# Three score tiles per burst beside denominators and values in a fused attention and FFN kernel

## The chip, the cores and the metric

The kernel runs on one core of one Trainium2 chip. The metric is the device time of one execution in microseconds (us), the median over several runs. The core has five engines with instruction queues of their own: TensorE (PE: matmuls, and PEld: its weight loads), VectorE (DVE), ScalarE (ACT), GpSimd (POOL) and SyncE (SP, which issues transfers). Each works through its own queue in order and waits on semaphores for the others.

## The reference

Attention with normalised queries and keys, and then a two-layer network with a leaky unit:

```python
q_n, k_n = rmsnorm(q, g_q), rmsnorm(k, g_k)          # x / sqrt(mean(x*x) + 1e-6) * g
scores = q_n @ k_n.T / sqrt(64)                      # per batch and head
attn   = softmax(scores)                             # over keys
x      = attn @ v            # -> (8*448, 12*64) tokens x model
h      = x @ w_in                                    # 768 -> 2048
g      = maximum(h, 0) + alpha * minimum(h, 0)
out    = g @ w_out                                   # 2048 -> 768
```

Sizes: 8 batches, 12 heads, 448 positions, 64 values per head; 3584 tokens, model width 768, inner width 2048. Inputs and output are float32 in memory; the matmuls run on float16.

## The kernel before

**Groups and tiles.** Four heads make a group `y`, so a batch has 3 groups (`G`) and the kernel 24 (`NG`). The 448 keys of a group are cut into 7 tiles of 64 (`J`). `score(y, j)` (L184) computes one score tile: four 64x64 matmuls that run side by side on quarters of the array, into a PSUM tile `sc` of which there are two. `soft(y, j)` (L198) is its exponential on ACT, from PSUM to `expT`.

**Around a group.** `load_qk` fetches queries and keys. `square` (L120; POOL, for the first two groups ACT), `reduce` (L130; DVE), `root` (L138; two small ACT instructions) and `scale` (L147; POOL, three of them on DVE) normalise them. `turn` (L157) transposes them on PE into the PSUM tile `acc`, and two DVE copies take them to `qT` and `kT`. When all seven tiles of a group are exponentiated, `den` (L221) sums them over keys by 28 matmuls with ones, into `acc`; `log` and `invert` (L225, L230) on ACT make the reciprocal. `attv` (L234) multiplies by the values, 28 matmuls into `acc` again, and a DVE multiply (L240) writes `xT`. There is a single `acc` buffer for turns, denominators and values.

**The network.** For every batch there are 16 `up` units (L245: six matmuls into a PSUM tile `hT`, then `ah` on ACT at L257 and `gT` on DVE at L258) and, per two batches, 14 `down` units (L262: sixteen matmuls into `op`, a DVE copy to `osb`, every second one with two output transfers on SP). `hT` and `op` share two PSUM buffers. A `down` can carry `jobs`, which it issues between its matmuls and its copy.

**The order.** Everything is issued in an order written out by hand (`tc.manual_schedule()`), so the loop at L413 decides each engine's queue. The loop runs over bursts `n`. A burst scores two tiles; in the burst after a group's last tile it also does that group's denominators, in the next one its values:

```python
dens = {last(y) + 1: y for y in range(NG)}
avs = {last(y) + 2: y for y in range(NG)}
```

Behind the matmuls of a burst stand its exponentials, the logarithm, roots and scales that are due (`roots`), a turn (`turns`), and then `gaps[n]`: the ups and downs that a small planner (L343 to L377) puts there. It goes by fixed costs per unit (`UP`, `DOWN`) and per burst (`cost(n)`). `invert` is issued behind the burst's second up. `prep` and `post` hold loads, squares and reduces by burst. Before the first batch's values are complete there are no ups; there `spin` (L284) issues idle matmuls in place of them, four in a plain burst and one in others. What is left after the last burst is in `rest`.

Of the kernel before, what the change touches and what calls it, by code (L numbers as in the profile page):

```python
# [21 lines left out]
def kernel(  # L22
# [14 lines left out]
    B, H, S, D = q.shape  # L37
    DM = H * D
    DF = moe_w_in.shape[1]
    J = S // 64  # L40
    HH = H // 2
    G = HH // 2
# [4 lines left out]
    NG = B * G  # L47
# [59 lines left out]
    def load_w_in(c):  # L107
        nc.gpsimd.dma_start(
            out=w_in_sb[:, :, ts(c, FB)],
            in_=moe_w_in[:, ts(c, FB)].rearrange("(k p) f -> p k f", p=128),  # L110
        )
# [45 lines left out]
    def turn(y):  # L157

        ps = psa.tile([128, 2, 512], FP32, name="tps", tag="acc")
        tps = [  # L160
            ps[:, n, : S].bitcast(FP16).rearrange("p (j c) -> p j c", j=J)
            for n in range(2)
        ]
        for tp, nm in zip(tps, "qk"):
            for j in range(J):
                nc.tensor.transpose(  # L166
                    tp[:, j, :], qs[y, nm][:, j].rearrange("p h d -> p (h d)"), ident
                )
        for tp, nm in zip(tps, "qk"):
            t = att.tile([128, 2, J, 64], FP16, name=f"{nm}T", tag=f"{nm}T", bufs=3)  # L170
            o = t.rearrange("p g j c -> p j g c")
            i4 = tp.rearrange("p j (g c) -> p j g c", g=2)
            if nm == "q":
                nc.vector.tensor_copy(out=o, in_=i4)
            else:
                nc.vector.tensor_scalar(  # L176
                    out=o, in0=i4, scalar1=gain[:, 0:1], scalar2=None, op0=ALU.mult
                )
            qkT[y, nm] = t
# [4 lines left out]
    def score(y, j):  # L184
        qT, kT = qkT[y, "q"], qkT[y, "k"]
        sc = pss.tile([128, 2, 512], FP32, name="sc", tag="sc")
        for par in range(2):
            for g in range(2):
                nc.tensor.matmul(  # L189
                    out=sc[ds(64 * g, 64), par, :S],  # L190
                    lhsT=kT[ds(64 * par, 64), g, j, :],
                    rhs=qT[ds(64 * par, 64), g].rearrange("p j c -> p (j c)"),
                    start=True,
                    stop=True,
                )
        scs[y, j] = sc

    def soft(y, j):  # L198
        if j == 0:
            expT[y] = att.tile([128, J, 2, S], FP16, name="expT", tag="expT")  # L200
        nc.scalar.activation(  # L201
            out=expT[y][:, j], in_=scs[y, j][:, :, :S], func=AF.Exp,
            scale=QK_SCALE, bias=expb[:, 0:1],
        )
# [16 lines left out]
    def den(y):  # L221
        dn = over_keys("dn", y, lambda g, par, j: ones[ds(64 * g, 64), :])
        rden[y] = dn

    def log(y):  # L225
        r = att.tile([128, 2, S], FP32, name="rden", tag="rden")
        nc.scalar.activation(out=r, in_=rden[y][:, :, :S], func=AF.Ln)  # L227
        rden[y] = r
# [5 lines left out]
    def attv(y):  # L234
        b, i = divmod(y, G)
        vv = vt[b]
        av = over_keys("av", y, lambda g, par, j: vv[ds(64 * g, 64), 2 * i + par, j, :])
        if i == 0:
            xT[b] = att.tile([128, 2, G, S], FP16, name="xT", tag="xT")
        nc.vector.tensor_mul(  # L240
            out=xT[b][:, :, i, :], in0=av[:, :, :S], in1=rden[y]
        )
# [41 lines left out]
    def spin(count):  # L284

        if count:
            ps = psf.tile([128, 512], FP32, name="spin", tag="mm")
            for _ in range(count):
                nc.tensor.matmul(  # L289
                    out=ps[:, :S], lhsT=ident, rhs=idle, start=True, stop=True  # L290
                )
# [1 line left out]

    NB = (NG * J + 1) // 2

    def last(y):
        return (J * y + J - 1) // 2

    dens = {last(y) + 1: y for y in range(NG)}
    avs = {last(y) + 2: y for y in range(NG)}
    prep, post, roots = {}, {}, {}

    def at(n, f, *a):
        prep.setdefault(max(int(n), 0), []).append((f, a))

    def after(n, f, *a):
        post.setdefault(max(int(n), 0), []).append((f, a))

    turn_at = [J * y // 2 - 1 for y in range(NG)]
    turns = {n: y for y, n in enumerate(turn_at) if y}
    jobs = {}
    for y in range(G, NG):

        n = turn_at[y - 1] if y < G + 2 else last(y - G) + 2
        at(n - 8, load_qk, y)
        for nm in "qk":
            at(n - 2, square, y, nm)
            if y < G + 2:  # L320
                after(n, reduce, y, nm)
            else:
                jobs.setdefault(n, []).append((reduce, (y, nm)))
        roots[n + 1] = y
    for b in range(1, B):
        at(J * G * b / 2 - 4, load_v, b)


    UP, DOWN = 1.13, 2.6
# [2 lines left out]
    for b in range(B):  # L332
        ups = [(UP, up, (b, ft)) for ft in range(NF)]
        odd = b % 2
        new = [
            (DOWN, down, (b - odd, t, oh))
            for t in (range(3, J) if odd else range(3)) for oh in range(2)
        ]
        tail = len(new) if b == B - 1 else 2 + odd
        periods.append((ups, carry, new[:tail]))  # L340
        carry = new[tail:]

    def cost(n):  # L343
        return 0.75 + (1.35 if n in dens or n in avs else 0.0) + (0.9 if n in turns else 0.0)

    first = last(G - 1) + 2
    gaps = [[] for _ in range(NB + 2)]
    for b in range(B - 1):
        lo = last(G * b + G - 1) + 2
        hi = last(G * b + 2 * G - 1) + 2  # L350
        ups, old, new = (list(u) for u in periods[b])
        mlp = sum(u[0] for u in ups + old + new)
        per = (mlp + sum(cost(n) for n in range(lo, hi))) / (hi - lo)
        clock = 0.0
        for n in range(lo, hi):
            clock += cost(n)
            free = n in avs or n in turns
            while ups or old or new:
                if old and (free or not ups):
                    u = old.pop(0)  # L360
                elif ups:
                    u = ups.pop(0)
                else:
                    u = new.pop(0)
                gaps[n].append(u[1:])
                clock += u[0]
                free = False
                ahead = 0.5 * (UP if ups else DOWN)
                if n < hi - 1 and clock + ahead > per * (n - lo + 1):
                    break  # L370
    ups, old, new = periods[B - 1]
    rest = []
# [30 lines left out]
                reduce(y, nm)  # L403
    for c in range(4):
        load_w_in(c)
        at(8 + 2 * c, load_w_out, c)
    after(0, root, 1)
    for nm in "qk":
        after(0, scale, 1, nm)
        after(2, reduce, 2, nm)  # L410
    roots[3] = 2

    for n in range(NB + 2):  # L413
        for f, a in prep.get(n, ()):
            f(*a)
        tiles = [divmod(m, J) for m in (2 * n, 2 * n + 1) if m < NG * J]
        for t in tiles:
            score(*t)
        if n in dens:
            den(dens[n])  # L420
        if n in avs:
            attv(avs[n])

        plain = n not in dens and n not in avs and n not in turns
        wait = plain and gaps[n] and gaps[n][0][0] is up
        late = []
        for t in tiles[:1] if wait else tiles:
            soft(*t)
        if wait:
            late = [(1, soft, t) for t in tiles[1:]]  # L430
        if n in dens:
            log(dens[n])
            late = [(2, invert, (dens[n],))]
        if n in roots:
            y = roots[n]
            root(y)
            for nm in "qk":
                scale(y, nm)
        if n in turns:
            turn(turns[n])  # L440
        done = 0
        for f, a in gaps[n]:
            if f is down:
                down(*a, jobs.pop(n, ()))
            else:
                f(*a)
                done += 1
                if late and done == late[0][0]:
                    for _, g, c in late:
                        g(*c)  # L450
                    late = []
        for _, g, c in late:
            g(*c)
        if n < first:
            spin(4 if plain else 1)
        for f, a in jobs.pop(n, []) + post.get(n, []):
            f(*a)
    for f, a in rest:
# [31 lines left out]
```

## Time and profile before

| | |
|---|---|
| median of 6 runs | 483.55 us (482.03 to 484.67) |
| the profiled execution's own time | 484.84 us |
| its span, first to last instruction | 483.1 us |
| PE matmul busy | 452.7 us, 4074 matmuls |
| ACT busy | 289.2 us; exponentials 160.3 us (168 of 1003 ns) |
| DVE busy | 217.2 us |
| POOL busy | 167.0 us |
| mean granted TensorE clock | 0.985 |
| first `up` starts | 51.86 us |

Durations that the profile gives for matmuls overlap, as they are pipelined: the distance from one start to the next is what one of them costs. "Idle before, releaser" names what ended an engine's wait.

### The profile page before, as it was taken

The page shows a single profiled execution, that of the slowest core. Times are in us where ns is not written, and L with a number is a line of the kernel's source. Part 1 is how long each engine was busy: PE and PEld are TensorE (multiplying, and loading weights), DVE is VectorE, ACT ScalarE, POOL GpSimd, SP SyncE. Part 2 cuts the span into 40 slices and gives each one's busy share as a digit, 9 for nine tenths or more (in the row PEclk, how much of TensorE's full clock was granted, in tenths as well). Part 3 has the DMA queues.
Part 4 walks back from the last instruction along what each step waited for, and adds up shares of the span by engine and source line. Part 5 has one row for each costly group of instructions (what it writes and reads, how often), then busy time and mean ns, then how long its engine had stood idle before and what let it go on. Part 6 is the DMA issues. An engine that isn't in the chain of part 4 may idle for free.

```text
span 483.1 us, 9494 instructions
## 1 busy us (share of the span) xinstructions
PE 452.7 (94%) x4074; PEld 235.4 (49%) x4074; DVE 217.2 (45%) x312; ACT 289.2 (60%) x399; POOL 167.0 (35%) x123
## 2 busy tenths in 40 slices
PE   6778899999999999999999999999999999999995
PEld 3243444555445454555545554554545554555463
DVE  2843554455354455355363353554462443334421
ACT  3788788757755756656764757558675558423300
POOL 3677636552352260541532442522613200000000
PEclk9797999999999999999999999999999999999999
DMA  7999997250705344423704425414501110111122
GB/s 191 197 256 228 239 215 135 62 142 18 168 0 122 99 110 58 110 66 79 156 11 110 110 74 95 106 43 103 92 1 34 35 34 1 34 34 33 34 65 66
DMA packets 32187, 45.46 MB, mean 94 GB/s; under 512 B 5008, under 2 KB 28560, under 8 KB 32144
## 3 DMA queue, kind: packets, MB, share of 16 engines
q1 hardware_dynamic: 19792, 32.13, 25.5%
q0 software_dynamic: 11776, 11.80, 15.6%
q10 hardware_dynamic: 576, 0.92, 0.6%
q8 instruction: 32, 0.52, 0.5%
q14 instruction: 11, 0.09, 0.1%
HBM read 45.62 MB, written 11.01 MB: 117 GB/s over the span
## 4 chain that ended last, share of the span: by engine, by line
PE 70%; ACT 12%; DVE 8%; issue 4%; POOL 3%; DMA 2%; SPq 0%; POOLq 0%; DVEq 0%; ACTq 0%
PE op L266 30%; PE hT L249 19%; PE sc L189 6%; ACT ah L257 6%; PE av L212 6%; PE dn L212 5%; DVE gT L258 4%; ACT expT L201 3%; DVE ss L133 3%; PE tps L166 3%; DMA nat<-in_k_dram 2%; POOL sq L127 1%; POOL qs L150 1%; PE spin L289 1%; ACT rden L227 1%
## 5 line engine op out<-in xcount | busy, mean ns | idle before, releaser
L201 ACT ACTIVATE expT<-sc,expb 128x896 f16<-128x896 f32 x168 | 160.3, 1003 | 51.2 <-PE sc L189 51.1
L249 PE MATMUL hT<-xT,w_in_sb 128*128 128x448 f16 x768 | 159.9, 353 | 8.0 <-DVE gT L258 6.5
L266 PE MATMUL op<-w_out_sb,gT 128*128 128x384 f16 x896 | 153.4, 327 | 1.7 <-DVE gT L258 1.7
L257 ACT ACTIVATE ah<-hT,alpha_sb 128x448 f16<-128x448 f32 x128 | 80.6, 634 | 97.3 <-PE hT L249 96.4
L258 DVE TENSOR_TENSOR gT<-hT,ah 128x448 f16<-128x448 f32 x128 | 79.5, 624 | 123.5 <-ACT ah L257 123.2
L150 POOL TENSOR_TENSOR qs<-nat,rr 128x896 f16<-128x896 f32 x45 | 75.0, 1687 | 128.9 <-ACT rr L145 105.1
L266 PEld LDWEIGHTS <-gT 128*128 128x128 f16 x896 | 85.1, 98 | 64.4 <-issue 11.2
L249 PEld LDWEIGHTS <-w_in_sb 128*128 128x128 f16 x768 | 72.4, 97 | 86.0 <-issue 26.2
L127 POOL TENSOR_TENSOR sq<-nat 128x896 f32<-128x896 f32 x44 | 72.9, 1677 | 86.8 <-DVE ss L133 86.8
L278 DVE COPY osb<-op 128x384 f32<-128x384 f32 x56 | 31.1, 555 | 86.6 <-PE op L266 86.6
L189 PE MATMUL sc<-qT,kT 64*64 64x448 f16 x672 | 52.2, 375 | 9.0 <-DVE kT L176 4.1
L133 DVE TENSOR_REDUCE ss<-sq 128x14 f32<-128x896 f32 x48 | 49.7, 1076 | 8.1 <-ACT sq L125 8.1
L240 DVE TENSOR_TENSOR xT<-av,rden 128x896 f16<-128x896 f32 x24 | 26.2, 1091 | 31.0 <-PE av L212 31.0
L212 PE MATMUL av<-expT,vt 64*64 64x448 f16 x672 | 36.0, 350 | 1.1 <-ACT rden L227 1.1
L212 PE MATMUL dn<-expT,ones 64*64 64x448 f16 x672 | 36.9, 356 | 0.0
L189 PEld LDWEIGHTS <-kT 64*64 64x64 f16 x672 | 13.8, 106 | 42.1 <-issue 31.8
L166 PE MATMUL tps<-ident,qs 128*128 128x128 f16 x336 | 23.7, 222 | 4.0 <-POOL qs L150 3.6
L212 PEld LDWEIGHTS <-vt 64*64 64x64 f16 x672 | 20.0, 107 | 13.4 <-issue 2.2
L212 PEld LDWEIGHTS <-ones 64*64 64x64 f16 x672 | 20.2, 110 | 12.9 <-issue 1.7
L166 PEld LDWEIGHTS <-qs 128*128 128x128 f16 x336 | 19.1, 99 | 12.9 <-issue 5.6
L227 ACT ACTIVATE rden<-dn 128x896 f32<-128x896 f32 x24 | 22.1, 920 | 4.2 <-PE dn L212 4.2
L232 ACT ACTIVATE rden<-rden 128x896 f32<-128x896 f32 x24 | 22.6, 943 | 0.3
(25 smaller groups left out, 98.9 us busy)
## 6 DMA issues: line engine op xcount, KB each, us to landing
out_dram<-osb SPq DMA_DIRECT2D x56, 192.0 KB, 2.7
nat<-in_q_dram SPq DMA_DIRECT2D x46, 224.0 KB, 3.9
nat<-in_k_dram SPq DMA_DIRECT2D x46, 224.0 KB, 5.0
vt<-in_v_dram POOLq DMA_DIRECT2D x16, 336.0 KB, 5.5
w_in_sb<-in_moe_w_in_dram POOLq DMA_DIRECT2D x4, 768.0 KB, 18.7
w_out_sb<-in_moe_w_out_dram POOLq DMA_DIRECT2D x4, 768.0 KB, 14.2
nat<-in_q_dram ACTq DMA_DIRECT2D x2, 224.0 KB, 6.4
nat<-in_k_dram ACTq DMA_DIRECT2D x2, 224.0 KB, 8.0
```

Source lines behind the costliest of these rows:

```text
L127: nc.gpsimd.tensor_mul(out=sqf, in0=src, in1=src)
L133: nc.vector.tensor_reduce(out=ss_t[y][:, "qk".index(nm)].rearrange("p h j -> p (h j)").unsqueeze(2), in_=sqs[y, nm], axis=AXIS_X, op=ALU.add,)
L150: eng.tensor_mul(out=t.rearrange("p j h d -> p h j d"), in0=nat[y, nm], in1=rr_t[y][:, "qk".index(nm)].unsqueeze(3).broadcast_to((128, 2, ...
L166: nc.tensor.transpose(tp[:, j, :], qs[y, nm][:, j].rearrange("p h d -> p (h d)"), ident)
L189: nc.tensor.matmul(out=sc[ds(64 * g, 64), par, :S], lhsT=kT[ds(64 * par, 64), g, j, :], rhs=qT[ds(64 * par, 64), g].rearrange("p j c -> p ...
L201: nc.scalar.activation(out=expT[y][:, j], in_=scs[y, j][:, :, :S], func=AF.Exp, scale=QK_SCALE, bias=expb[:, 0:1],)
L212: nc.tensor.matmul(out=acc[ds(64 * par, 64), g, :S], lhsT=weights(g, par, j), rhs=e[ds(64 * g, 64), j, par, :], start=(j == 0), stop=(j == ...
L249: nc.tensor.matmul(out=hT[:, :S], lhsT=w_in_sb[:, c, ts(ft, 128)], rhs=x[:, c, :], start=(c == 0), stop=(c == KM - 1),)
L257: nc.scalar.activation(out=ah, in_=hT[:, :S], func=AF.Copy, scale=alpha_sb[:, ft : ft + 1])
L258: nc.vector.tensor_max(out=gT[:, ft, ds((b & 1) * S, S)], in0=hT[:, :S], in1=ah)
L266: nc.tensor.matmul(out=op[:, :OH], lhsT=gT[:, ft, ts(t, 128)], rhs=w_out_sb[:, ft, ds(oh * OH, OH)], start=(ft == 0), stop=(ft == NF - 1),)
L278: nc.vector.tensor_copy(out=o[:, ds(oh * OH, OH)], in_=op[:, :OH])
```

## The change

The list of bursts is now built ahead. A burst in which denominators or values are due takes three tiles, others take two. The third is scored behind the denominators or values, and its exponential is issued behind the other two. A batch thus has 7.5 bursts where it had 10.5 (six with three tiles, 1.5 with two). With the bursts everything that is counted in them is placed anew:

- a turn is issued behind the first up or down of its burst, not before it, and it never shares a burst with denominators; mostly it shares one with values;
- reduces stand in the burst of another group's denominators: carried by that burst's first `down` if it has one, else at its end; loads, squares and roots are counted from there;
- the transfers of `w_out` and of the values are issued in other bursts;
- every burst of the prologue has four spin matmuls;
- the planner's cost of a burst depends on its tiles, and its units are distributed over fewer bursts.

```diff
-    NB = (NG * J + 1) // 2
-    def last(y):
-        return (J * y + J - 1) // 2
-    dens = {last(y) + 1: y for y in range(NG)}
-    avs = {last(y) + 2: y for y in range(NG)}
+    bursts, dens, avs, first_in, last_in = [], {}, {}, {}, {}
+    m = 0
+    while m < NG * J or len(avs) < NG:
+        n = len(bursts)
+        if len(dens) > len(avs):
+            avs[n] = len(avs)
+        elif len(dens) < NG and last_in.get(len(dens), n) < n:
+            dens[n] = len(dens)
+        count = min(3 if n in dens or n in avs else 2, NG * J - m)
+        bursts.append([divmod(m + c, J) for c in range(count)])
...
-    turn_at = [J * y // 2 - 1 for y in range(NG)]
+    turn_at = {
+        y: max(n for n in range(first_in[y]) if n not in dens) for y in range(1, NG)
+    }
...
-        n = turn_at[y - 1] if y < G + 2 else last(y - G) + 2
-        at(n - 8, load_qk, y)
+        n = max(d for d in dens if d <= turn_at[y] - 2)
+        at(n - 5, load_qk, y)
         for nm in "qk":
             at(n - 2, square, y, nm)
-            if y < G + 2:
-                after(n, reduce, y, nm)
-            else:
-                jobs.setdefault(n, []).append((reduce, (y, nm)))
+            jobs.setdefault(n, []).append((reduce, (y, nm)))
...
-        return 0.75 + (1.35 if n in dens or n in avs else 0.0) + (0.9 if n in turns else 0.0)
+        return (
+            0.31 + 0.19 * len(bursts[n])
+            + (1.35 if n in dens or n in avs else 0.0) + (0.9 if n in turns else 0.0)
+        )
...
-        at(8 + 2 * c, load_w_out, c)
+        at(7 + c, load_w_out, c)
...
-        for t in tiles:
+        for t in tiles[:2]:
             score(*t)
+        plain = n not in dens and n not in avs
+        wait = plain and gaps[n] and gaps[n][0][0] is up
+        for t in tiles[:1] if wait else tiles[:2]:
+            soft(*t)
         if n in dens:
             den(dens[n])
         if n in avs:
             attv(avs[n])
+        for t in tiles[2:]:
+            score(*t)
+            soft(*t)
...
-        if n in turns:
-            turn(turns[n])
         done = 0
-        for f, a in gaps[n]:
+        for k, (f, a) in enumerate(gaps[n]):
...
+            if k == 0 and n in turns:
+                turn(turns[n])
...
         if n < first:
-            spin(4 if plain else 1)
+            spin(4)
```

More of the change, by code (lines that the diff above doesn't have):

```diff
@@ L291, in spin @@
                 )
-    NB = (NG * J + 1) // 2
-    def last(y):
-        return (J * y + J - 1) // 2
-    dens = {last(y) + 1: y for y in range(NG)}
-    avs = {last(y) + 2: y for y in range(NG)}
+    bursts, dens, avs, first_in, last_in = [], {}, {}, {}, {}
[8 more added lines that the diff above has]
+        bursts.append([divmod(m + c, J) for c in range(count)])
+        for y, j in bursts[n]:
+            first_in.setdefault(y, n)
+            if j == J - 1:
+                last_in[y] = n
+        m += count
+    NB = len(bursts)
+    den_at = {y: n for n, y in dens.items()}
+    av_at = {y: n for n, y in avs.items()}
     prep, post, roots = {}, {}, {}
@@ L309, in after @@
         post.setdefault(max(int(n), 0), []).append((f, a))
-    turn_at = [J * y // 2 - 1 for y in range(NG)]
-    turns = {n: y for y, n in enumerate(turn_at) if y}
+    turn_at = {
+        y: max(n for n in range(first_in[y]) if n not in dens) for y in range(1, NG)
+    }
+    turns = {n: y for y, n in turn_at.items()}
     jobs = {}
     for y in range(G, NG):
-        n = turn_at[y - 1] if y < G + 2 else last(y - G) + 2
-        at(n - 8, load_qk, y)
+        n = max(d for d in dens if d <= turn_at[y] - 2)
+        at(n - 5, load_qk, y)
         for nm in "qk":
             at(n - 2, square, y, nm)
-            if y < G + 2:
-                after(n, reduce, y, nm)
-            else:
-                jobs.setdefault(n, []).append((reduce, (y, nm)))
+            jobs.setdefault(n, []).append((reduce, (y, nm)))
         roots[n + 1] = y
     for b in range(1, B):
-        at(J * G * b / 2 - 4, load_v, b)
+        at(av_at[G * b] - 4, load_v, b)
     UP, DOWN = 1.13, 2.6
@@ L338 @@
         ]
-        tail = len(new) if b == B - 1 else 2 + odd
+        tail = len(new) if b == B - 1 else 2 if odd or b == 0 else 1
         periods.append((ups, carry, new[:tail]))
@@ L343, in cost @@
     def cost(n):
-        return 0.75 + (1.35 if n in dens or n in avs else 0.0) + (0.9 if n in turns else 0.0)
-    first = last(G - 1) + 2
-    gaps = [[] for _ in range(NB + 2)]
+        return (
+            0.31 + 0.19 * len(bursts[n])
+            + (1.35 if n in dens or n in avs else 0.0) + (0.9 if n in turns else 0.0)
+        )
+    first = av_at[G - 1]
+    gaps = [[] for _ in range(NB)]
     for b in range(B - 1):
-        lo = last(G * b + G - 1) + 2
-        hi = last(G * b + 2 * G - 1) + 2
+        lo, hi = av_at[G * b + G - 1], av_at[G * b + 2 * G - 1]
         ups, old, new = (list(u) for u in periods[b])
@@ L356 @@
             clock += cost(n)
-            free = n in avs or n in turns
+            free = True
             while ups or old or new:
@@ L368 @@
                 ahead = 0.5 * (UP if ups else DOWN)
-                if n < hi - 1 and clock + ahead > per * (n - lo + 1):
+                short = n in turns and len(gaps[n]) < 2
+                if n < hi - 1 and not short and clock + ahead > per * (n - lo + 1):
                     break
@@ L411 @@
     roots[3] = 2
-    for n in range(NB + 2):
+    for n in range(NB):
         for f, a in prep.get(n, ()):
             f(*a)
-        tiles = [divmod(m, J) for m in (2 * n, 2 * n + 1) if m < NG * J]
-        for t in tiles:
+        tiles = bursts[n]
+        for t in tiles[:2]:
             score(*t)
+        plain = n not in dens and n not in avs
+        wait = plain and gaps[n] and gaps[n][0][0] is up
+        for t in tiles[:1] if wait else tiles[:2]:
+            soft(*t)
         if n in dens:
@@ L422 @@
             attv(avs[n])
-        plain = n not in dens and n not in avs and n not in turns
-        wait = plain and gaps[n] and gaps[n][0][0] is up
+        for t in tiles[2:]:
+            score(*t)
+            soft(*t)
         late = []
-        for t in tiles[:1] if wait else tiles:
-            soft(*t)
         if wait:
@@ L451 @@
                     late = []
+            if k == 0 and n in turns:
+                turn(turns[n])
+        if not gaps[n] and n in turns:
+            turn(turns[n])
         for _, g, c in late:
```

## The prediction

> **What bounds the kernel now.** I read the page first: the engines' shares and the chain that ended last.
>
> ```profile
> PE 452.7 (94%) x4074; PEld 235.4 (49%) x4074; DVE 217.2 (45%) x312; ACT 289.2 (60%) x399; POOL 167.0 (35%) x123
> PE 70%; ACT 12%; DVE 8%; issue 4%; POOL 3%; DMA 2%; SPq 0%; POOLq 0%; DVEq 0%; ACTq 0%
> ```
>
> TensorE (PE) is the bound. Fewer bursts can save only what PE pays to enter and leave one, and any new hole in PE's row costs its full length. So I went to the timeline of one denominator burst in mid-kernel and the value burst behind it.
>
> ```profile
> 175.88 0.57 PE L189 MATMUL sc<-qT,kT 64*64 64x448 f16 x8
> ...
> 176.38 2.45 PE L249 MATMUL hT<-xT,w_in_sb 128*128 128x448 f16 x12
> ...
> 182.98 0.57 PE L189 MATMUL sc<-qT,kT 64*64 64x448 f16 x8
> 183.09 0.63 ACT L257 ACTIVATE ah<-hT,alpha_sb 128x448 f16<-128x448 f32 x1 [0.62 <-PE hT L249]
> 183.38 1.50 PE L212 MATMUL dn<-expT,ones 64*64 64x448 f16 x28
> 183.62 1.90 ACT L201 ACTIVATE expT<-sc,expb 128x896 f16<-128x896 f32 x2
> ...
> 184.81 2.44 PE L249 MATMUL hT<-xT,w_in_sb 128*128 128x448 f16 x12
> 185.40 0.93 ACT L227 ACTIVATE rden<-dn 128x896 f32<-128x896 f32 x1
> 186.19 0.65 ACT L257 ACTIVATE ah<-hT,alpha_sb 128x448 f16<-128x448 f32 x1
> ...
> 187.56 1.29 PE L249 MATMUL hT<-xT,w_in_sb 128*128 128x448 f16 x6 [0.30 <-DVE gT L258]
> 187.82 0.94 ACT L232 ACTIVATE rden<-rden 128x896 f32<-128x896 f32 x1
> 188.78 0.57 PE L189 MATMUL sc<-qT,kT 64*64 64x448 f16 x8
> 188.89 0.63 ACT L257 ACTIVATE ah<-hT,alpha_sb 128x448 f16<-128x448 f32 x1
> ```
>
> Starts matter here, since ends on PE are modelled. On PE: two score tiles 0.40 us (182.98 to 183.38), a plain burst 0.50 (175.88 to 176.38), so leaving it costs 0.10; six `hT` matmuls before a burst take 1.23 (187.56 to 188.78) where six among themselves take 1.13, so entering costs 0.10. A burst's fixed cost is 0.20 us. `dn` to the next `hT` is 1.43, so 1.33 without the leaving. An `up` is 1.13; a `down` (`op`, 16 matmuls) 2.61; a turn 0.79 (the chain's pieces). On ACT, start to start: exponential 0.89 (it lasts 1.00), logarithm 0.80 (185.40 to 186.19), `ah` 0.53, inverse 0.84 (82.11 to 82.95 elsewhere in the timeline). An `up` has its `ah` ready 1.33 after its start, and 1.37 after that `ah` starts its PSUM buffer is free (186.19 to 187.56).
>
> Even now there are holes: summed over all matmul starts, what exceeds these pitches is 19.3 us from 56.5 us on. The last `up` above is one (0.44): a third `up` in a row waits for the first one's buffer.
>
> **What is removed.** The built order shows 63 bursts instead of 86, of which 46 have three tiles; so the change does what it says. The state "28 tiles scored, fourth turn and two ups done" is the common mark: before, at 56.5 us, with 72 bursts to come; after, with 52. Removed: 20 x 0.20 = 3.9 us (0.195 unrounded). The third tile itself moves and costs its 0.20 in either place, if it does not wait.
>
> **The prologue.** Square 3 now stands before scale 2 on POOL. Now POOL idles 3.29 us ahead of scale 2 (26.36), and its squares and scales to 41.9 end the wait before the third turn. Walking the new order with 1.65 us for each square or scale, scale 3 ends at 38.2 and that turn no longer waits for it. ACT takes over. From its first exponential (16.1) to the start of the inverse of group 2 it has 25 exponentials (22.3), three logarithm-inverse steps (2.9), two inverses (1.7) and four roots (2.3): 29.2, and 4.3 of waiting, mostly for `kT` of groups 1 to 3, by the walk; so 49.6. The value matmuls start there too (the logarithm has freed the accumulator), the multiply 1.61 later, and `xT` of group 2 is ready at 52.3 instead of 53.15. The 16 added spin matmuls sit in PE's waits for ACT: cover enough, 0; uncovered, 16 x 0.19 = 3.0. Of the transfers, values of batch 1 are issued after the first w_out chunk (about 47 instead of 32.9); now the 768 KB chunks on that queue land 4 to 7.5 us after the one ahead, the last of w_in at 47.2, so they land near 57 and are read at 63: 0. If they took the 18.4 us that they take now, they would land at 65.4: +2.4. Two more tiles are then scored (-0.4), but turn 4 now has one `up` between it and the scores that read it, behind `gT` on DVE: `kT` ready at 56.1, wait 0.9. The mark is reached at 56.0, not 56.5: -0.5. Clock:
>
> ```profile
> 40.00:43.00 3.00, 1.98 (x22) 1.21 (x18) 0.34 (x2) 2.27 (x3) 2.60 (x3) 0.84 1.24 207
> 43.00:46.00 3.00, 2.58 (x13) 0.70 (x12) 3.00 (x4) 2.01 (x2) 0.90 (x1) 0.50 1.20 242
> 46.00:50.00 4.00, 4.00 (x46) 1.76 (x46) 0.01 (x1) 3.00 (x5) 3.98 (x4) 0.64 1.18 235
> ```
>
> In these windows (after PE, PEld, DVE, ACT and POOL: granted clock, DMA share, GB/s) the clock is half from 42.0 to 48.9, although PE was never idle for more than 0.5 us before it. There `dn` takes 2.25, four spins 1.61: some 2.2 us too many. With four spins in every burst I take full clock, as in 22 to 42; at half clock again: +2.2. [...]
>
> **What the new order adds.** Two score buffers serve three tiles: the third waits for the first exponential. Its place in a burst is +1.73 (0.40 + 1.33). With an `ah` ahead on ACT the exponential starts at +0.64 (182.98 to 183.62), ends at +1.64; the hand-over of 0.05 leaves 0.04 of cover: 0. I walked all bursts after the mark:
> - Where a denominator burst ends in `up`, then inverse, the inverse stands in front of the next burst's exponentials: start +0.64+0.84 = 1.48, third score at 2.53: 0.80 lost. Value bursts 20, 27, 35, 37, 42, 50, 52, 60: 8 x 0.80 = 6.4. Now the value burst has no third score, and nobody waits.
> - Where ups follow the denominators directly (11, 14, 21, 31, 46), a third exponential stands before logarithm and `ah`: the third PSUM user waits 0.99 (11, 21) or 1.19 instead of 0.44: 5.5 in all.
> - In 11, 14, 21 the two reduces (1.99) are put at the burst's end on DVE, ahead of the `xT` multiply; the turn that follows one `up` later needs that accumulator: 3 x 1.29 = 3.9.
> - Scores waiting for a fresh `kT` (0.25 or 0.05): 1.0.
> - Third ups in a row, as such holes are now: nine single ones of 0.44, four long runs with 0.73 (13, 23) or 0.89 (38, 53), two of 0.12, five of 0.42 in the rest at the end: 9.5.
>
> Sum 26.3, against 19.3 now: +7.0. Per two batches in mid-kernel the walk gives 110.9 us against a measured 110.9: there the saving is eaten exactly; the loss comes in the first two batches, where ups stand without downs.
>
> **Sum.** -3.9 - 0.5 + 7.0 = +2.6 us. Span 483.1 to 485.7; the profiled time 484.84 (1.7 outside the span, and 1.3 above the median) to 487.4; the median 483.55 to **486.1**.
>
> By "TensorEngine Tiling (Array Packing)", PSUM Bottleneck, tiled matmuls leave PSUM evacuation as the limit. An estimate by that rule, three exponentials (2.67) for each three-tile burst of 2.11, would be 46 x 0.56 = 26 us slower; the row says 0.04 of cover in most of them, and the sum goes by the row.
>
> **Rivals.** (1) Faster, about 479.7: the third score doesn't wait behind the inverse. If ACT runs ahead of PE there, as it does where a `down` comes between, the 6.4 falls away. It decides from where four of the eight waits are gone: then the sum is below zero. For it: ACT is busy 60% only. Against: ACT is in order, and the second `up` releases its `ah` only 0.11 us after the next burst's first score (188.78, 188.89).
> (2) A wash, 482.2 to 484.9: the holes are not additive. If the three waits behind the reduces vanish, 486.1 - 3.9 = 482.2; a third of that, 484.8. For it: while PE waits, ACT and DVE catch up, and my walk rounds every hand-over up. Against: the mid-kernel walk uses the same steps and has room for neither.
> (3) Slower than the sum, about 490: the cover of 0.04 fails, 38 other three-tile bursts losing 0.1 each, +3.8. For it: it is the thinnest cover here, and the hand-over of 0.05 is one reading; against: the starts repeat within 0.01.
>
> **Numbers.** The sum's case has 0.52 (484.9 to 488.5 by its own bounds: a cold prologue above, a few waits fewer below), rival 1 0.20, the wash 0.18, rival 3 0.10. Range 480.5 to 489.0: about half of rivals 1 and 3 lie outside. About 0.3% (1.45 us) is what a measurement of this kernel can tell from no change: faster 0.20, same 0.20 (the wash and the sum's lower edge), slower 0.60.
>
> **What would show it.** Right: PE's `sc` row gains waits on ACT `expT`, about eight of 0.8 us, each behind an L232-type inverse; turns of groups 5, 6 and 9 wait on DVE `xT`; mid-kernel still 110.9 us per two batches; first `up` ends near 53; clock full from 22 us on. Wrong: no `sc` wait on `expT` after 60 us (then rival 1), such a wait in most bursts (rival 3), or a half clock after 40 us.

## The result, and the profile after

The changed kernel takes 486.71 us (median of 22 runs, 484.94 to 487.48) against 483.52 us before (46 runs): a ratio of 1.0062, 95% interval 1.0051 to 1.0073. It is slower by 3.2 us. The profiled execution took 487.36 us, its span is 485.6 us, against 484.84 and 483.1 before.

The page's first block and its chain, of the changed kernel:

```profile
PE 449.2 (93%) x4090; PEld 242.8 (50%) x4090; DVE 218.5 (45%) x312; ACT 288.3 (59%) x399; POOL 167.4 (34%) x123
PE 70%; ACT 15%; DVE 8%; issue 3%; DMA 2%; POOL 0%; DVEq 0%
```

PE is busy 3.5 us less with 16 matmuls more, and the span is 2.5 us longer: PE has more holes (time between two matmul starts beyond the usual step). In the chain, POOL's 3% are gone (the prologue no longer hangs on its squares and scales) and ACT has 15% for 12%. Who makes PE wait is in the view of waits, PE alone (total, times, longest), first of the changed kernel, then of the one before:

```profile
PE sc L189 <- ACT expT L201: 7.3, 15, 0.6
PE hT L249 <- DVE gT L258: 7.1, 21, 1.0
PE tps L166 <- DVE xT L240: 4.4, 5, 1.1
```

```profile
PE hT L249 <- DVE gT L258: 6.5, 25, 0.3
...
PE sc L189 <- ACT expT L201: 1.9, 4, 0.5
PE op L266 <- DVE gT L258: 1.7, 6, 0.3
```

This view counts from the modelled ends of matmuls, so each wait looks shorter than the hole it makes between starts. The order of size is plain: scores wait for exponentials, single waits of an up have grown from 0.3 to 1.0, and turns wait for `xT`, for which the view of the kernel before has no row.

One such place is bursts 19 and 20, from the timeline of the changed kernel:

```profile
112.51 2.43 PE L249 MATMUL hT<-xT,w_in_sb 128*128 128x448 f16 x12
...
114.87 0.57 PE L189 MATMUL sc<-qT,kT 64*64 64x448 f16 x8
114.98 0.64 ACT L257 ACTIVATE ah<-hT,alpha_sb 128x448 f16<-128x448 f32 x1 [0.50 <-PE hT L249]
...
115.28 1.49 PE L212 MATMUL av<-expT,vt 64*64 64x448 f16 x28
115.51 0.94 ACT L232 ACTIVATE rden<-rden 128x896 f32<-128x896 f32 x1
...
116.35 2.80 ACT L201 ACTIVATE expT<-sc,expb 128x896 f16<-128x896 f32 x3
...
117.40 0.38 PE L189 MATMUL sc<-qT,kT 64*64 64x448 f16 x4 [0.63 <-ACT expT L201]
```

The second up's `ah` and the inverse stand ahead of the three exponentials, whose first ends at 117.35. The third score starts at 117.40, 2.53 after the burst's first and 0.80 after its place at 1.73.

And bursts 11 and 12, where the reduces come late:

```profile
61.73 1.29 PE L249 MATMUL hT<-xT,w_in_sb 128*128 128x448 f16 x6 [0.82 <-DVE gT L258]
...
64.27 2.07 DVE L133 TENSOR_REDUCE ss<-sq 128x14 f32<-128x896 f32 x2
...
64.97 1.31 PE L249 MATMUL hT<-xT,w_in_sb 128*128 128x448 f16 x6
...
66.26 1.08 DVE L240 TENSOR_TENSOR xT<-av,rden 128x896 f16<-128x896 f32 x1
...
67.39 0.78 PE L166 MATMUL tps<-ident,qs 128*128 128x128 f16 x11 [1.11 <-DVE xT L240]
```

The first line is the third up, late by 0.98 from start to start because a third exponential stands before logarithm and `ah`. The `xT` multiply starts when the second reduce lets it, and the turn starts when `xT` is done, 1.27 late.

The windows of the prologue (busy times of PE, PEld, DVE, ACT, POOL, then granted clock, DMA share, GB/s):

```profile
12.00:16.00 4.00, 1.90 (x18) 1.37 (x22) 2.81 (x5) 1.89 (x3) 2.02 (x3) 0.56 1.29 160
16.00:20.00 4.00, 4.00 (x24) 1.12 (x24) 2.88 (x3) 3.24 (x5) 3.03 (x2) 0.58 1.24 208
20.00:40.00 20.00, 16.17 (x210) 8.13 (x212) 11.91 (x13) 17.07 (x23) 18.24 (x14) 1.00 1.15 241
40.00:60.00 20.00, 17.02 (x213) 8.98 (x206) 7.68 (x10) 17.32 (x24) 16.18 (x14) 1.00 1.17 238
```

The half clock near 42 to 49 us, which the profiled execution before had, is absent; the earlier one (12.5 to 19.3 us here, 14.7 to 21.6 before) is there in both.

### The profile page after: what moved, and what is told of

Its sections match the earlier page's. It is cut to its first block, busy times and chain, and to the rows that moved or that the text cites. A ratio compares the mean times of both kernels' runs of the same rounds, so it can differ in the third digit from the quotient of the medians.

```text
span 485.6 us, 9537 instructions
## 1 busy us (share of the span) xinstructions
PE 449.2 (93%) x4090; PEld 242.8 (50%) x4090; DVE 218.5 (45%) x312; ACT 288.3 (59%) x399; POOL 167.4 (34%) x123
## 4 chain that ended last, share of the span: by engine, by line
PE 70%; ACT 15%; DVE 8%; issue 3%; DMA 2%; POOL 0%; DVEq 0%
PE op L266 31%; PE hT L249 21%; ACT expT L201 7%; PE sc L189 6%; ACT ah L257 5%; PE dn L212 5%; PE tps L166 4%; DVE gT L258 4%; PE av L212 3%; DMA nat<-in_q_dram 2%; DVE ss L133 2%; ACT rden L232 2%; DVE xT L240 1%; DVE kT L176 1%; DVE qT L174 1%
## 5 line engine op out<-in xcount | busy, mean ns | idle before, releaser
L201 ACT ACTIVATE expT<-sc,expb 128x896 f16<-128x896 f32 x168 | 157.5, 1006 | 23.4 <-PE sc L189 23.2
L189 PE MATMUL sc<-qT,kT 64*64 64x448 f16 x672 | 54.2, 366 | 11.2 <-ACT expT L201 7.3
L189 PEld LDWEIGHTS <-kT 64*64 64x64 f16 x672 | 18.6, 105 | 43.8 <-issue 31.9
L212 PE MATMUL dn<-expT,ones 64*64 64x448 f16 x672 | 35.9, 349 | 0.0
L166 PEld LDWEIGHTS <-qs 128*128 128x128 f16 x336 | 21.1, 99 | 12.3 <-issue 5.5
```

What stands on the lines that cost most here:

```text
L166: nc.tensor.transpose(tp[:, j, :], qs[y, nm][:, j].rearrange("p h d -> p (h d)"), ident)
L189: nc.tensor.matmul(out=sc[ds(64 * g, 64), par, :S], lhsT=kT[ds(64 * par, 64), g, j, :], rhs=qT[ds(64 * par, 64), g].rearrange("p j c -> p ...
L201: nc.scalar.activation(out=expT[y][:, j], in_=scs[y, j][:, :, :S], func=AF.Exp, scale=QK_SCALE, bias=expb[:, 0:1],)
L212: nc.tensor.matmul(out=acc[ds(64 * par, 64), g, :S], lhsT=weights(g, par, j), rhs=e[ds(64 * g, 64), j, par, :], start=(j == 0), stop=(j == ...
```

## The experiments

Medians swing with the clock in the prologue, so beside each median stands a second number: the time from the first `hT` matmul to the last matmul's start in the profiled execution, which has no prologue in it. All edited kernels but the last start from the changed one. Each ratio is to runs of the kernel before that were timed beside that kernel (medians 483.32 to 483.68).

| kernel | median us | ratio to before, interval | first up to last matmul, us |
|---|---|---|---|
| before | 483.5 | | 425.7 |
| changed | 486.71 | 1.0062 (1.0051 to 1.0073) | 427.9 |
| inverse first | 479.72 | 0.9921 (0.9903 to 0.9939) | 421.3 |
| reduces early | 483.03 | 0.9986 (0.9973 to 1.0000) | 424.2 |
| third exponential later | 483.43 | 0.9995 (0.9980 to 1.0011) | 424.8 |
| the three together | 473.68 | 0.9792 (0.9771 to 0.9812) | 414.4 |
| third tile in a burst of its own | 480.39 | 0.9942 (0.9921 to 0.9962) | 422.6 |
| up, down, up, up | 470.91 | 0.9748 (0.9723 to 0.9774) | 412.7 |
| spins as before | 487.37 | 1.0085 (1.0055 to 1.0115) | 427.9 |
| before, four spins everywhere | 482.96 | 0.9992 (0.9977 to 1.0006) | 425.7 |

**The inverse, first.**

```diff
-            late = [(2, invert, (dens[n],))]
+            if gaps[n] and gaps[n][0][0] is down:
+                invert(dens[n])
+            else:
+                late = [(2, invert, (dens[n],))]
```

> The changed kernel (486.7 us), with the inverse issued right behind the logarithm in every denominator burst whose first unit is a down, instead of behind its second up. Theory (in-order walk, eight value bursts in which the third score waits 0.80 us because the inverse stands ahead of the exponentials): the eight waits go, nothing comes in their place since ACT is idle during the down; 486.7 - 6.4 = 480.3, below the kernel before. Rival (holes are not additive; ACT or DVE is late again one burst on): at most half of it comes back, 483.5 or more.

Measured: 479.72. Waits of PE in this kernel, scores on exponentials:

```profile
PE sc L189 <- ACT expT L201: 2.3, 7, 0.5
```

That is eight waits fewer than the 15; the seven left stand in the prologue. From first up to last matmul 427.9 became 421.3: 6.6 for an expected 6.4. The rival, that another wait takes their place, falls.

**Reduces early.**

```diff
+        if n in dens and gaps[n] and not any(f is down for f, _ in gaps[n]):
+            for f, a in jobs.pop(n, []):
+                f(*a)
         done = 0
```

> The changed kernel, with the reduces of bursts 11, 14 and 21 (those with ups alone beside denominators) issued on DVE ahead of the burst's ups instead of behind them. Theory: squares are long there, DVE is idle at that point, the three waits of a turn for xT (1.27 each) go; 486.7 - 3.8 = 482.9. Rival (the turn would be late anyway, or the gT of the ups now waits for the reduces): no change, 486.7.

Measured: 483.03; from first up to last matmul 3.7 less. Waits of PE in this kernel, turns on `xT`:

```profile
PE tps L166 <- DVE xT L240: 1.0, 2, 0.5
```

The three long waits of a turn are gone (4.4, five times, up to 1.1 in the changed kernel; the two left stand in the prologue); two holes of 0.05, at the third up of bursts 12 and 22, are new.

**The third exponential, later.**

```diff
+        defer = n in dens and gaps[n] and gaps[n][0][0] is up
         for t in tiles[2:]:
             score(*t)
-            soft(*t)
+            if not defer:
+                soft(*t)
...
                 done += 1
+                if defer and done == 1:
+                    for t in tiles[2:]:
+                        soft(*t)
```

> The changed kernel, with the third tile's exponential issued behind the logarithm and the first up's ah in the five bursts 11, 14, 21, 31 and 46, where ups follow the denominators directly. Theory: the third PSUM user's wait of 0.98 (two bursts) and 1.18 (three) falls to the 0.41 of any third up in a row; for bursts 31 and 46, where the third user is a down, likewise; 486.7 - 3.4 = 483.3. Rival (the wait is set by ups in a row alone, not by the third exponential): 486.7.

Measured: 483.43; from first up to last matmul 3.1 less. Waits of PE in this kernel, ups on `gT`:

```profile
PE hT L249 <- DVE gT L258: 5.2, 21, 0.2
```

The longest was 1.0 in the changed kernel. The five holes are 0.41 now. Three new ones of 0.07 show in value bursts 12, 15 and 22: there the third up now starts so early that the inverse ahead of its `ah` makes that 0.10 late (0.21 after the next burst's first score, not 0.11), the exponentials with it, and the cover of 0.04 is used up.

**All three together.**

> The three edits together. Theory (each wait has a place of its own, so the parts add): 486.7 - 6.4 - 3.8 - 3.4 = 473.1, that is 2.1% faster than the kernel before, whose saving of bursts then shows. Rival (shared slack, the next wait comes up): 476.5 or more.

Measured: 473.68. The parts by themselves give 6.6 + 3.7 + 3.1 = 13.4 from first up to last matmul; together 13.5. They add. Waits of PE in this kernel:

```profile
PE hT L249 <- DVE gT L258: 5.2, 21, 0.2
...
PE sc L189 <- ACT expT L201: 1.7, 6, 0.4
...
PE tps L166 <- DVE xT L240: 1.0, 2, 0.5
```

With the three kinds of wait gone it is 2.1% faster than the kernel before. Not all of that is saved bursts. From first up to last matmul it gains 11.3 on the kernel before (425.7 to 414.4). Its holes over 0.04 come to 13.8 there, those of the kernel before to 20.2, so 6.4 of the 11.3 is waiting that the kernel before had too, and 4.9 is the rest, of which fewer bursts are most. No run took the holes out of the kernel before and left its 86 bursts, so what that alone would bring is not shown.

**The third tile in a burst of its own** (the first two edits, and this one; it also defers that tile's exponential behind the first unit's, as the third edit does):

```diff
-        for t in tiles[2:]:
+        split = tiles[2:] if gaps[n] else []
+        for t in [] if split else tiles[2:]:
             score(*t)
             soft(*t)
...
+            if k == 0:
+                for t in split:
+                    score(*t)
+                    soft(*t)
             if k == 0 and n in turns:
```

> The kernel with the three edits (473.7 us), but in the 41 bursts that have three tiles and units behind them the third tile is scored behind the first unit, as a burst of its own; nothing is added but 41 entries and exits of the 64x64 tiles. Theory (a burst's fixed cost is 0.195 us, whatever it holds): 41 x 0.195 = 8.0, and up to 1.2 more in burst 16, where the next burst's second score now waits for that tile's exponential; 481.7 to 482.9. Rival (the fixed cost is mostly hidden, so that the change saved nothing by fewer bursts): under 476.

Measured: 480.39, 6.7 above the three edits, below the 8.0 expected in the medians; from first up to last matmul 8.2 more. The holes over 0.04 in that stretch fell by 1.2 (13.8 to 12.6: fewer ups follow each other directly, but burst 16 gets its 1.07), and one tile more, burst 10's third, now falls inside the stretch (0.2). So 41 entries and exits cost 8.2 + 1.2 - 0.2 = 9.2, or 0.22 each. A lone tile between downs takes 0.41 in this trace where the third tile of a burst takes 0.19, which says the same. The rival, a hidden fixed cost, falls; that the cost of a lone tile is that of a burst with two or three is not shown by it.

**Up, down, up, up** (the three edits, and this one):

```diff
+    for n in range(NB):
+        g = gaps[n]
+        if n not in dens and n not in avs and [u[0] for u in g[:4]] == [down, up, up, up]:
+            g[0], g[1] = g[1], g[0]
```

> The kernel with the three edits (473.7 us), and in the five plain bursts that hold a down and then three ups (28, 33, 43, 48, 58) the order up, down, up, up. Theory (the third up in a row waits 0.41 for the first one's PSUM buffer; with a down between them the buffer is free in time): five waits go, 473.7 - 2.0 = 471.7. Rival (the wait moves to the first up, which now follows the ups of the burst before, or to the second exponential, which is issued behind the first up): 473.7.

Measured: 470.91, 2.8 less; from first up to last matmul 1.6 less, which is four holes of 0.41. The fifth burst, 58, holds four ups, so three still follow the down: the expectation had overlooked that. Against the runs of the kernel before that were timed beside each, the medians differ by 2.4 (12.4 less, where the three edits had 10.0 less). The 0.8 beyond the four holes is not accounted for; the prologue's clock alone moves a run by more. This is the fastest version, 2.5% under the kernel before.

**Spins as before.**

```diff
-            spin(4)
+            spin(4 if plain and n not in turns else 1)
```

> The changed kernel with the spin matmuls of the prologue as before: four in bursts 0, 1, 3 and 8, one in the other six, 18 fewer than 40. Theory (the spins sit in waits of PE for ACT): they cost nothing, 486.7, if the clock stays full after its first half-clock stretch. By the row of the kernel before (half clock with PE busy but full of short waits) the half clock comes back near 40 us, and with it up to 2.2 us: 488.9. Rival (18 spins are on PE's path): 486.7 - 18 x 0.19 = 483.3.

Measured: 487.37 (485.98 to 490.72 in six runs). That the spins lie on PE's path (483.3) is excluded. In the profiled execution, of 490.72, the half clock comes back:

```profile
28.00:31.00 3.00, 1.84 (x25) 0.84 (x28) 1.33 (x2) 2.97 (x4) 3.00 (x3) 0.99 1.15 272
31.00:41.00 10.00, 8.18 (x83) 4.27 (x75) 4.29 (x5) 5.58 (x8) 9.37 (x7) 0.50 1.19 251
```

The first up starts at 55.6 instead of 52.2, and from there on nothing differs (427.9 both). The medians of the two kernels cannot be told apart, but the clocks can: four of the six executions have a mean granted clock of 0.982 to 0.988, and none of the 22 of the changed kernel is below 0.990. So in the changed kernel the added spins do keep the clock up more often; what that is worth in the median these six runs are too few to say.

**The kernel before, with four spins in every prologue burst.**

```diff
-            spin(4 if plain else 1)
+            spin(4)
```

> The kernel before (483.5 us) with four spin matmuls in each of its twelve prologue bursts, 48 instead of 24. Theory (its half-clock stretch from 42.0 to 48.9 us comes from too little work on PE, and costs 2.2): the clock stays full there and the time falls to 481.3, less what spins cost that are not covered. Rival (the half clock has nothing to do with the spins, or the prologue's path is elsewhere): 483.5, or up to 24 x 0.19 = 4.6 more if they stand on PE's path.

Measured: 482.96 beside 483.50; the interval of the ratio holds 1. The gain of 2.2 is missed. In the profiled execution there is no half clock after 18.0 us, and the first up starts at 50.0 instead of 51.9:

```profile
14.60:18.00 3.40, 2.96 (x20) 0.85 (x20) 2.37 (x3) 2.29 (x4) 1.95 (x2) 0.50 1.37 152
18.00:50.00 32.00, 27.93 (x350) 13.72 (x343) 15.03 (x16) 27.53 (x36) 25.53 (x20) 1.00 1.18 242
```

Of these 1.9 us, 0.4 are there already at the first score (15.0 instead of 15.4) and still 0.4 at 41.5; the other 1.4 come where the half clock of the kernel before stood. So there that stretch cost about 1.4, not 2.2, and it did not set the typical time. In 50 executions of the kernel before that were timed beside these experiments, the nine with a mean clock up to 0.986 have a median of 484.5, 27 around 0.991 one of 483.7, and 14 from 0.994 one of 482.4. The profiled execution of the kernel before (0.985) is of the kind of the nine. Of the twelve executions with added spins one is up to 0.986, which does not tell them from nine in 50.

## Why the prediction was right

**The forecast.** 486.1 was predicted, 486.7 measured; a span of 485.7, and 485.6 found. The likeliest case was the one that came. That the span came out within 0.1 is partly luck: the prologue gave 0.4 less than its term, the holes were 0.2 smaller, and all else shrank by some 0.2 more than the bursts' 3.9.

**Holes.** The sum over the holes was 26.3 from the mark on; found are 26.1. By kind: eight waits behind the inverse, 0.80 each, in the bursts named; five third PSUM users at 0.98 or 1.18; three turns at 1.27; scores for a fresh `kT` at 0.25. The sizes of the first three kinds were then confirmed, each by the edit that took it away; the waits for `kT` were read from the trace alone. Per two batches in mid-kernel, one repeating place (the `down` after two ups, 202.01 and 312.76) gives 110.75 us, against 110.85 before (197.35 and 308.20), as predicted: the saving is eaten there.

**Bursts.** From first up to last matmul the change costs 427.9 - 425.7 = +2.2. Holes there grew from 20.2 to 27.1, so all else shrank by some 4.8. Two score tiles fewer are left after the first up (0.4), and 21 bursts fewer at 0.195 make 4.1: 0.3 is left over. The term of 3.9 (20 bursts) stands.

**The prologue.** Its mechanism was right: no wait for POOL before the third turn, ACT as the limit, `xT` of group 2 at 52.7 for a predicted 52.3, the first up's end near 53.5. The size was off: the mark is reached at 56.35 instead of 56.0, so -0.1 for -0.5. About 0.5 of it lies before any part of the new order: the first score already starts at 16.0 instead of 15.4. The values of batch 1 landed at 59.1, not at 57, and were read at 63.4: no wait.

**Profiled and typical execution.** The sum was made from one execution and carried to the median one to one. That execution lies 1.3 above the median of its kernel, the profiled one of the changed kernel only 0.65 above its own. By the mean clocks, the half-clock stretch near 42 us was in that execution, but not in most. Between profiles the change costs 2.5, between medians 3.2; in executions with a clock from 0.994 on it costs 2.7 (485.1 against 482.4), around 0.991 3.4 (487.1 against 483.7). The step that failed by 0.6 is this carrying over.

**The clock and the page.** The sum took full clock, with 2.2 as a bound, and the clock did stay full from 19.3 us on. What sets off a half clock is open. In the kernel before it began at 42.0 us with PE busy 2.00 of the 3.41 us ahead and no wait over 0.51. In the kernel with spins as before it began at 31.0 us, after three microseconds in which PE was busy 1.84 of 3.00, again with no wait over 0.51. The Trainium skill, "TensorE: Matmul & The Clock Gate", gives under "HAM oscillation" the rule to have no idle gaps of PE over about 3.4 us; that rule does not account for these two stretches. The same page tells, under "A second HAM failure mode", of a kernel whose clock oscillates because PE idles briefly but often, and gives no figure for how often; whether the two stretches are of that kind no run here shows.

**The rivals.** Rival 1 (ACT ahead of PE, so no wait behind the inverse) had no case: the wait is there eight times out of eight. The wash fell with the additivity of the edits. Rival 3, the cover of 0.04: it held in the changed kernel, where no three-tile burst loses 0.1, and failed by 0.07 in three bursts as soon as one edit let an inverse push an `ah` by 0.10. The estimate of 26 us by the Trainium skill's "TensorEngine Tiling (Array Packing)", PSUM Bottleneck, took as a rule what that page calls possible ("PSUM copy may become bottleneck"); what came of it were the eight waits behind an inverse, 6.4 us, with ACT busy 59% of the span.

## What to carry to other kernels

Fewer entries and exits on a bound engine are worth their fixed cost times their number (here 0.20 us each by the start times of neighbours, 0.22 by experiment). What a merged burst puts into the in-order queues of the other engines is worth as much: walk the queue of each engine through one period, because a long instruction that used to be harmless (an inverse, a reduce) may now stand ahead of one that the bound engine waits for. Once such a walk gives each hole a cause, some can be cured by moving a line or two: here three small edits took away 13.4 of 27.1 us, and the cures added. Look for holes in the kernel before as well, or the cure is credited to the change.

## What was not expected of the hardware

The spread between executions of one kernel, about 4 us (481.4 to 485.5), goes with the mean granted clock: from 0.994 on the kernel before takes 482.4, up to 0.986 484.5. In all ten traces the clock is full from 49 us until after the last matmul, so by these traces the difference is made in the prologue. There the half clock came in stretches of 3.4, 6.8 or 10.2 us, at different times in each execution.

There are two kinds of stretch. Nine of the ten traces have one that begins between 11.7 and 14.8 us, during PE's wait for the first scaled queries or up to 2.4 us behind it; that wait lasted 1.9 to 3.7 us in them. The tenth (reduces early, mean clock 1.0) waited 0.96 us there and had no half clock in the prologue at all; its first up starts at 50.2 instead of 52.2. The other kind, at 42.0 us in the kernel before and at 31.0 us with spins as before, began although no wait in the 3.4 us ahead of it was over 0.51 us. The share of time that PE was busy does not tell when such a stretch begins: with spins as before PE was busy 1.97 of 3.42 us before the one at 31.0, but only 1.83 of 3.41 from 44.6 to 48.0, and kept full clock after that.
